# A transformer block on one core: first chunk's q and k stored straight into the attention layout, and the opening loads in the order of need

## Chip, core and metric

The kernel runs on one core of one Trainium2 chip. The metric is the device time of one execution, in microseconds (us). Besides it I quote the *span* of a profiled execution, which is some 2 us shorter, because the trace's times belong to it. The engines are named as the profile names them: PE (matrix), PEld (its weight load), DVE (vector), ACT (scalar), POOL (GpSimd), SP (SyncE, which here only issues DMAs), and the core's 16 DMA engines. The *granted clock* is the share of PE's full clock that the chip allowed it. Each timed execution is marked with a state, by its time and granted clock; those timed in rounds are all marked fast.

## The reference, cut to what matters

```python
def A(x, wqkv, wo):               # x is 2048 x 1024, 32 heads of 32
    q, k, v = split(x @ wqkv)     # wqkv is 1024 x 3072
    idx = pos[:, None] - 2 * arange(8)            # 8 keys, each 2 tokens further back
    attn = softmax(where(idx >= 0, q . k[idx] * scale, -1e9))
    return (attn . v[idx]) @ wo
def B(x, w_gate, w_up, w_down):   # 1024 -> 3584 -> 1024
    return ((x @ w_gate) * (x @ w_up)) @ w_down
h = x + A(layernorm(x), wqkv, wo)
return h + B(layernorm(h), w_gate, w_up, w_down)
```

All inputs and outputs are bfloat16.

## The kernel before

The tokens go through in four chunks of 512. For each chunk: layer norm, q/k/v projection on PE, attention on DVE, output projection ("wo"), second layer norm, gated feed-forward. PE should never stop. The attention and the later layer norms therefore run as *background generators*: after each group of matmuls (1.73 us) the program hands out credit, and background instructions are written into the program as long as the credit lasts. So the program order of DVE, ACT and SP work relative to PE's matmuls is fixed when the kernel is built.

```python
    def step(self, us):                                  # class Background
        self.now += us
        self.credit = min(self.credit + us * self.rate, 4.0)
        while self.credit > 0:
            item = next((i for i in self.items if i[0] <= self.now), None)
            ...
            got = next(item[1])                          # emit the generator's next piece
            if isinstance(got, tuple):
                item[0] = self.now + got[1]              # ("later", us)
            else:
                self.credit -= got
# ---- opening: what SP loads, in this order
    load_x0(0); load_x0(1)
    load_w(2)                 # weight block 0 in two halves
    load_x0(2)
    load_w(2)                 # weight block 1, ahead of the last x tile
    load_x0(3)
# ---- layer norm of a later chunk; the pool behind normalize() has 4 "ln" buffers
    def ln1(c):
        xts = load_x(c, "x", nc.gpsimd)
        yield "later", 8.0 if c < 3 else 5.0
        lnTs[c] = lnTp.tile([128, KO, TC], BF, tag="lnT", name=f"lnT1_{c}")
        def norm(t):
            ln = normalize(xts[t], mv4, rs4, t)          # DVE
            nc.sync.dma_start_transpose(lnTs[c][:, :, bass.ts(t, 128)], ln[:])
        for t in range(4):
            stats(xts[t], mv4, t)                        # DVE
            rstd_of(mv4, rs4, t, t + 1)                  # two steps on ACT
            ...
# ---- after each group of a projection: PSUM -> staging tile -> DRAM
    def evac_qkv(c, m, ps):                              # m: 0-7 q, 8-15 k, 16-23 v
        sg = t1k.tile([128, HB + TC], BF, tag="t1k", name=f"sg{c}_{m}")
        nc.scalar.copy(sg[:, HB:HB + TC], ps[:])
        hg = m % 8
        if m < 8:
            nc.sync.dma_start(qd[c][:, 4 * hg:4 * hg + 4, :, :].rearrange("c g d s -> (g d) c s"),
                              sg[:, HB:HB + TC].rearrange("p (c s) -> p c s", c=4))
            return
        nc.scalar.copy(sg[:, 0:HB], halo[:, m - 8, :])   # last 16 tokens of the chunk before
        if c + 1 < NCH:
            nc.scalar.copy(halo[:, m - 8, :], ps[:, TC - HB:TC])
        ...                                              # k and v likewise, to kd[c], vd[c]
# ---- and back, into the attention's layout (partition = sub-chunk x head)
    def load_qk(c):
        nc.gpsimd.dma_start(qD[:], qd[c].rearrange("c g d s -> (c g) d s"))
        nc.gpsimd.dma_start(kD[:], kd[c].rearrange("c g d s -> (c g) d s"))
    def attention(c):
        if c == 0:
            load_qk(0)
            load_v(0)
            yield "later", 7.0
        ...                                              # DVE: logits, softmax, weighted v
        nc.gpsimd.dma_start(od[c].rearrange("c g d s -> (c g) d s"), oD[:])
        ...                                              # od -> oT, the input of wo
# ---- program order
    qkv(0, range(1, 6))
    bg.add(ln1(3))
    start_attention(0)
    qkv(1, range(6))
    ...
    bg.finish(atts[0])
    bg.rate = 0.98
    nxt = wo_ln2(0)
```

PE's groups share 8 PSUM banks, and ACT frees a bank by copying it to `sg`. ACT also takes the layer norms' two inverse-square-root steps and the attention's exponential, in program order with those copies. And SP issues nearly everything: weights, stores, transposing DMAs.

## Time and profile before

| | before |
|---|---|
| time, median of 3 (lowest to highest) | 813.2 us (813.04 to 814.09) |
| profiled span, granted clock | 812.0 us, 0.995 |
| first projection at full width starts | 20.2 us |
| first attention product on DVE | 67.8 us |
| output projection of chunk 0 starts | 165.3 us |
| output projection of chunk 3 starts, after a wait of 4.9 us | 491.5 us |

The prediction shows the page and PE's waits. For what follows two more views are needed. First, SP's own row in the timeline: start, duration, queue, line, kind of DMA, target and source, count.

```profile
23.99 11.76 SPq L265 DMA_DIRECT2D qd<-sg  x8
...
54.43 6.66 SPq L209 DMA_TRANSPOSE lnT<-ln  x2
```

Eight stores took SP 11.76 us. A transposing DMA took SP 1.3 us at the least and 2.3 in the median; this pair, beside a load of the attention's inputs, took 6.66.

### The profile page before, as it was taken

The numbers are of one execution on the slowest core, as the hardware profiler recorded it, in microseconds if no ns is written. First come the engines' busy times: TensorE is split into PE (matmuls) and PEld (weight loads), VectorE is DVE, ScalarE is ACT, GpSimd is POOL, SyncE is SP. The second block draws the span as 40 slices with busy tenths as digits, with TensorE's granted clock in tenths as the row PEclk, the third lists the DMA queues.
The fourth block names the chain that finished last, engine by engine and source line by source line (L and its number), as shares of the span: only waits on it lengthen the run. The fifth ranks groups of instructions, "written<-read, shape, count | busy, mean of one in ns | idle before, by whom it ended". The sixth has DMA issues, their size and how long they took to land.

```text
span 812.0 us, 9901 instructions
## 1 busy us (share of the span) xinstructions
PE 795.3 (98%) x3700; PEld 410.6 (51%) x3769; DVE 551.8 (68%) x580; ACT 254.9 (31%) x562; POOL 171.8 (21%) x172
## 2 busy tenths in 40 slices
PE   7999999999999999999999997999999999999998
PEld 5444444444444444444444443466666666644445
DVE  4538999999899898999989945635646565311111
ACT  2554444314333310023333100245545555400000
POOL 3100000200001000002000001497878778100000
PEclk9999999999999999999999998999999999999999
DMA  9999564999855948848564596533323233465600
GB/s 310 317 254 235 123 192 105 260 281 253 289 161 189 316 117 277 281 132 288 182 199 145 136 312 141 129 99 84 103 54 104 55 102 90 152 219 182 187 27 27
DMA packets 194448, 144.32 MB, mean 178 GB/s; under 512 B 83424, under 2 KB 188000, under 8 KB 192352
## 3 DMA queue, kind: packets, MB, share of 16 engines
q1 hardware_dynamic: 189856, 118.51, 52.5%
q0 software_dynamic: 4544, 25.17, 8.9%
q8 instruction: 30, 0.49, 0.3%
q14 instruction: 18, 0.15, 0.1%
HBM read 114.29 MB, written 22.02 MB: 168 GB/s over the span
## 4 chain that ended last, share of the span: by engine, by line
PE 83%; issue 13%; DMA 3%; SPq 0%; POOL 0%; DVE 0%; ACT 0%; POOLq 0%
PE ps L343 19%; PE acc L524 18%; PE pg L343 7%; PE pu L343 7%; PE pz L575 6%; PE py L575 6%; PE px L575 6%; PE wo L466 5%; PE pv L575 3%; PE accl L514 3%; DMA od<-oD 1%; DMA x<-in_A_x_dram 1%; DMA oT<-od 1%; POOL oT L443 0%; SPq L226 0%
## 5 line engine op out<-in xcount | busy, mean ns | idle before, releaser
L343 PE MATMUL ps<-lnT,w_qkv 128*128 128x512 bf16 x721 | 158.4, 379 | 0.8
L343 PEld LDWEIGHTS <-w_qkv 128*128 128x128 bf16 x736 | 72.0, 98 | 86.6
L343 PE MATMUL pg<-lnT,w_wg 128*128 128x512 bf16 x439 | 105.0, 379 | 0.5
L343 PE MATMUL pu<-lnT,w_wu 128*128 128x512 bf16 x439 | 104.9, 379 | 0.4
L524 PE MATMUL acc<-w_wd,gs 128*128 128x512 bf16 x439 | 96.7, 379 | 0.5
L262 ACT CAST sg<-ps 128x512 bf16<-128x512 f32 x96 | 55.5, 586 | 65.3 <-PE ps L343 59.0
L506 DVE TENSOR_TENSOR h<-acc,h 128x512 bf16<-128x512 f32 x28 | 17.4, 682 | 81.8 <-PE acc L524 81.8
L428 DVE TENSOR_TENSOR pv<-vD,at 128x4096 bf16<-128x4096 bf16 x32 | 72.4, 2287 | 0.4
L388 DVE TENSOR_TENSOR prod<-qD,kD 128x4096 bf16<-128x4096 bf16 x32 | 72.3, 2285 | 0.0
L524 PEld LDWEIGHTS <-gs 128*128 128x128 bf16 x448 | 43.9, 98 | 52.8
L343 PEld LDWEIGHTS <-w_wg 128*128 128x128 bf16 x448 | 43.8, 98 | 52.9
L343 PEld LDWEIGHTS <-w_wu 128*128 128x128 bf16 x448 | 43.8, 98 | 52.9
L466 PE MATMUL wo<-w_wo,oT 128*128 128x512 bf16 x251 | 58.4, 392 | 5.1 <-DMA oT<-od 4.9
L491 ACT CAST gs<-pg 128x512 bf16<-128x512 f32 x56 | 32.8, 586 | 91.5 <-PE pg L343 88.1
L440 POOL DMA_DIRECT2D od<-oD x4 | 2.2, 544 | 251.0 <-DVE oD L438 153.5
L575 PE MATMUL px<-lnT,w_pair 128*128 128x512 bf16 x210 | 52.5, 380 | 0.9
L496 ACT CAST us<-pu 128x512 bf16<-128x512 f32 x56 | 32.8, 586 | 60.1 <-PE pu L343 54.4
L551 POOL TENSOR_TENSOR sw<-w_pair 128x512 fp32r<-128x512 bf16 x28 | 36.5, 1302 | 60.5 <-issue 32.2
L466 PEld LDWEIGHTS <-oT 128*128 128x128 bf16 x256 | 25.7, 101 | 37.4 <-DMA oT<-od 5.4
L178 ACT ACTIVATE rs<-mv,eps 128x1 f32<-128x1 f32 x32 | 9.4, 294 | 104.6 <-DVE mv L175 99.7
L553 POOL TENSOR_TENSOR sw<-w_pair 128x512 fp32r<-128x512 bf16 x28 | 36.9, 1318 | 0.0
L390 DVE TENSOR_TENSOR prod<-prod 128x4096 bf16<-128x4096 bf16 x16 | 36.6, 2289 | 0.3
(128 smaller groups left out, 1066.1 us busy)
## 6 DMA issues: line engine op xcount, KB each, us to landing
w_wd<-in_B_w_down_dram SPq DMA_DIRECT2D x32, 896.0 KB, 6.2
w_wg<-in_B_w_gate_dram SPq DMA_DIRECT2D x14, 1024.0 KB, 8.1
w_wu<-in_B_w_up_dram SPq DMA_DIRECT2D x14, 1024.0 KB, 6.0
w_wo<-in_A_wo_dram SPq DMA_DIRECT2D x8, 1024.0 KB, 6.9
w_pair<-in_B_w_gate_dram SPq DMA_DIRECT2D x14, 512.0 KB, 4.0
w_pair<-in_B_w_up_dram SPq DMA_DIRECT2D x14, 512.0 KB, 5.4
kd<-sg SPq DMA_DIRECT2D x32, 144.0 KB, 3.3
vd<-sg SPq DMA_DIRECT2D x32, 144.0 KB, 2.7
```

The costliest lines, as they stand in the source:

```text
L262: nc.scalar.copy(sg[:, HB:HB + TC], ps[:])
L343: nc.tensor.matmul(ps[:], lhsT=wt[:, ko, bass.ts(j, 128)], rhs=rhs[:, ko, :], start=(ko == 0), stop=(ko == KO - 1))
L388: nc.vector.tensor_tensor(prod[:, j], qD[:], kD[:, :, o:o + SUB], ALU.mult)
L390: nc.vector.tensor_tensor(prod[:, :, 0:16], prod[:, :, 0:16], prod[:, :, 16:32], ALU.add)
L428: nc.vector.tensor_tensor(pv[:, j], vD[:, :, o:o + SUB], at[:, w, None, :].to_broadcast((128, DH, SUB)), ALU.mult)
L466: nc.tensor.matmul(ps[:], lhsT=oTs[c][:, kk, t, :], rhs=wts["wo", c, hf][:, kk, :], start=(kk == 0), stop=(kk == KO - 1))
L491: nc.scalar.copy(gs[:], pg[:])
L496: nc.scalar.copy(us[:], pu[:])
L524: nc.tensor.matmul(acc[t][:], lhsT=hT[f][:, bass.ts(t, 128)], rhs=wts["wd", c, hf, b][:, j, :], start=(f == 0), stop=(f == NF - 1))
L551: nc.gpsimd.tensor_tensor(sw[:, 0], a21, a22, ALU.add)
L553: nc.gpsimd.tensor_tensor(sw[:, 2], a11, a21, ALU.subtract)
L575: nc.tensor.matmul(ps[:], lhsT=lhs[:, ko, :], rhs=rhs[:, ko, :], start=(fresh and ko == 0), stop=(ko == 3), skip_group_check=not fresh)
```

## The change

The intent has two parts. Chunk 0's q and k skip DRAM: each staged tile goes by four DMAs of four destination partitions each straight into `qD` or `kD`, half issued by SP and half by POOL, so that attention 0 can start sooner. And the opening's loads come in the order of need: the fourth x tile ahead of the second weight block, then weight blocks and x tiles alternating, all on SP. Along with it, layer norms and attention 0 move forward in program order, and the first transposed tile is split into two PSUM tiles.

```diff
+    qkv_in = {("q", 0): att.tile([128, DH, SUB], BF, tag="qD", name="qD0"),
+              ("k", 0): att.tile([128, DH, SUB + HB], BF, tag="kD", name="kD0")}
     def evac_qkv(c, m, ps):
...
+        if c == 0 and m < 16:
+            dst, o, n = (qkv_in["q", 0], HB, SUB) if m < 8 else (qkv_in["k", 0], 0, SUB + HB)
+            for cp in range(4):
+                (nc.sync if cp % 2 else nc.gpsimd).dma_start(
+                    dst[cp * 32 + 4 * hg:cp * 32 + 4 * hg + 4, :, :],
+                    sg[:, o + cp * SUB:o + cp * SUB + n])
+            return
... opening loads
     load_x0(0)
     load_x0(1)
-    load_w(2)
+    load_w0(0, 4)
     load_x0(2)
-    load_w(2)
+    load_w0(4, 4)
     load_x0(3)
... after the first projection
-    pump()
+    w1 = wpool.tile([128, KO, 512], BF, tag="w", name="w_qkv_1")
+    nc.gpsimd.tensor_copy(w1[:, 0, 0:1], x0[3][:, 0:1])
+    pump(2, w1)
+    xtiles[1] = load_x(1, "x", nc.sync)
+    pump(3)
+    xtiles[2] = load_x(2, "x", nc.sync)
+    pump(6)
... layer norm: no delay; chunk 3's transposes wait until chunk 0's projection is written
-        yield "later", 8.0 if c < 3 else 5.0
... program order
-    qkv(0, range(1, 6))
+    qkv(0, range(1, 4))
     bg.add(ln1(3))
     start_attention(0)
+    qkv(0, range(4, 6))
+    emitted.add("qkv0")
+    load_v(0)
     qkv(1, range(6))
     start_attention(1)
+    pump(pair_at)
```

More of the change, by code (lines that the diff above doesn't have):

```diff
@@ L154, with pump @@
     wts = {}
-    state = {"next": 0, "live": 0, "limit": pair_at}
-    def pump(eng=None):
+    state = {"next": 0, "live": 0, "limit": 1}
+    def pump(limit=None, wt=None):
+        state["limit"] = limit or state["limit"]
         while state["next"] < state["limit"] and state["live"] < 7:
             key, src, n = stream[state["next"]]
-            wt = wpool.tile([128, KO, 512], BF, tag="w", name="w_" + "_".join(map(str, key)))
-            (eng or nc.sync).dma_start(wt[:, 0:n, :], src)
+            if wt is None:
+                wt = wpool.tile([128, KO, 512], BF, tag="w", name="w_" + "_".join(map(str, key)))
+            nc.sync.dma_start(wt[:, 0:n, :], src)
             wts[key] = wt
+            wt = None
             state["next"] += 1
@@ L199, with transpose @@
     lnTs = {}
+    xtiles = {}
+    emitted = set()
     def ln1(c):
-        xts = load_x(c, "x", nc.gpsimd)
-        yield "later", 8.0 if c < 3 else 5.0
-        lnTs[c] = lnTp.tile([128, KO, TC], BF, tag="lnT", name=f"lnT1_{c}")
+        if c == 2:
+            xtiles[3] = load_x(3, "x", nc.gpsimd)
+        xts = xtiles[c]
         mv4, rs4 = ln_tiles(f"1_{c}")
+        lns = [None] * 4
+        def transpose(t):
+            if c not in lnTs:
+                lnTs[c] = lnTp.tile([128, KO, TC], BF, tag="lnT", name=f"lnT1_{c}")
+            nc.sync.dma_start_transpose(lnTs[c][:, :, bass.ts(t, 128)], lns[t][:])
         def norm(t):
-            ln = normalize(xts[t], mv4, rs4, t)
-            nc.sync.dma_start_transpose(lnTs[c][:, :, bass.ts(t, 128)], ln[:])
+            lns[t] = normalize(xts[t], mv4, rs4, t)
+            if c < 3:
+                transpose(t)
         for t in range(4):
@@ L219, in ln1, with load_w0 @@
         yield 0.55
-    def load_w(parts=1):
-        key, src, n = stream[state["next"]]
-        wt = wpool.tile([128, KO, 512], BF, tag="w", name="w_" + "_".join(map(str, key)))
-        for q in range(parts):
-            nc.sync.dma_start(wt[:, bass.ts(q, KO // parts), :], src[:, bass.ts(q, KO // parts), :])
-        wts[key] = wt
-        state["next"] += 1
-        state["live"] += 1
+        if c == 3:
+            while "qkv0" not in emitted:
+                yield "later", 1.0
+            for t in range(4):
+                transpose(t)
     x0 = [hp.tile([128, D], BF, tag="h", name=f"x0_{t}") for t in range(4)]
+    w0 = wpool.tile([128, KO, 512], BF, tag="w", name="w_qkv_0")
+    wts["qkv", 0] = w0
+    state["next"] += 1
+    state["live"] += 1
     def load_x0(t):
         nc.sync.dma_start(x0[t][:], x[bass.ds(t * 128, 128), :])
+    def load_w0(lo, n):
+        nc.sync.dma_start(w0[:, lo:lo + n, :], wqkv_v[:, lo:lo + n, 0:512])
     load_x0(0)
     load_x0(1)
-    load_w(2)
+    load_w0(0, 4)
     load_x0(2)
-    load_w(2)
+    load_w0(4, 4)
     load_x0(3)
@@ L263, in evac_qkv @@
         hg = m % 8
+        if m >= 8:
+            nc.scalar.copy(sg[:, 0:HB], halo[:, m - 8, :])
+            if c + 1 < NCH:
+                nc.scalar.copy(halo[:, m - 8, :], ps[:, TC - HB:TC])
+        if c == 0 and m < 16:
[5 more added lines that the diff above has]
+            return
         if m < 8:
@@ L267, in evac_qkv @@
             return
-        nc.scalar.copy(sg[:, 0:HB], halo[:, m - 8, :])
-        if c + 1 < NCH:
-            nc.scalar.copy(halo[:, m - 8, :], ps[:, TC - HB:TC])
         dst = (kd, vd)[m // 8 - 1][c]
@@ L298, in first_transpose @@
     def first_transpose(t):
-        pts[t] = psum.tile([128, KO, 128], BF, tag="mm", name=f"pt{t}")
-        for kk in range(KO):
-            nc.tensor.transpose(pts[t][:, kk, :], lns[t][:, bass.ts(kk, 128)], ident[:])
-        nc.scalar.copy(lnTs[0][:, 0:4, bass.ts(t, 128)], pts[t][:, 0:4, :])
+        for hf in range(2):
+            pt = psum.tile([128, KO // 2, 128], BF, tag="mm", name=f"pt{t}_{hf}")
+            for kk in range(KO // 2):
+                nc.tensor.transpose(pt[:, kk, :], lns[t][:, bass.ts(4 * hf + kk, 128)], ident[:])
+            pts[t, hf] = pt
+        nc.scalar.copy(lnTs[0][:, 0:4, bass.ts(t, 128)], pts[t, 0][:])
     def first_copy(t):
-        nc.vector.tensor_copy(lnTs[0][:, 4:8, bass.ts(t, 128)], pts[t][:, 4:8, :])
+        nc.vector.tensor_copy(lnTs[0][:, 4:8, bass.ts(t, 128)], pts[t, 1][:])
     def first_mm(t, kos):
@@ L331 @@
     first_mm(3, range(8))
-    order_after_x0 = const.tile([128, 1], BF)
-    nc.gpsimd.tensor_copy(order_after_x0[:], x0[3][:, 0:1])
-    pump()
+    w1 = wpool.tile([128, KO, 512], BF, tag="w", name="w_qkv_1")
[5 more added lines that the diff above has]
+    pump(6)
     bg.add(ln1(1))
@@ L356 @@
     oTs = {}
-    qkv_in = {}
     stored = set()
@@ L377, in attention @@
     def attention(c):
-        if c == 0:
-            load_qk(0)
-            load_v(0)
-            yield "later", 7.0
-        qD, kD, vD = qkv_in["q", c], qkv_in["k", c], qkv_in["v", c]
+        qD, kD = qkv_in["q", c], qkv_in["k", c]
         lg = att.tile([128, W, SUB], F32, tag="lg", name=f"lg{c}")
@@ L418, in attention @@
         prefetch_qk(c + 1)
+        while ("v", c) not in qkv_in:
+            yield "later", 1.0
+        vD = qkv_in["v", c]
         at = att.tile([128, W, SUB], BF, tag="at", name=f"at{c}")
```

## The prediction

> **What bounds the kernel now.** I read the page's busy shares first, then TensorE's (PE's) waits, then the chain that ended last around the longest of them, then the stretches by window, and last the timeline of the opening.
>
> The page, busy shares and slices:
> ```profile
> PE 795.3 (98%) x3700; PEld 410.6 (51%) x3769; DVE 551.8 (68%) x580; ACT 254.9 (31%) x562; POOL 171.8 (21%) x172
> ...
> PE   7999999999999999999999997999999999999998
> ...
> PEclk9999999999999999999999998999999999999999
> ```
> PE is the bound: 795.3 of 812.0 us. The two slices with a 7 (of 20.3 us each) are the opening and a place near 490 us; the second also has the only clock digit below 9. Removing every idle moment would give at most 16.7 us, 2.1%, plus what the slow clock costs. So "within 2%" is nearly settled at once; the question is how much of that the change gets.
>
> PE's waits, whole span:
> ```profile
> PE wo L466 <- DMA oT<-od: 4.9, 1, 4.9
> PE pt L301 <- DVE ln L183: 2.4, 3, 1.3
> PE ps L310 <- ACT lnT L302: 1.4, 4, 0.7
> ```
> One wait of 4.9 us, for the last chunk's attention output; the others, 3.8 us, lie in the first 20 us.
>
> The chain that ended last:
> ```profile
> 165.43 6.26 PE wo L466 x29
> 171.75 7.50 PE wo L466 x34
> ...
> 476.19 9.13 DMA od<-oD
> 485.90 5.53 DMA oT<-od
> 491.47 12.04 PE wo L466 x42
> 503.56 4.70 PE wo L466 x21
> ```
> VectorE (DVE) ends attention of chunk 3 at about 475; out to DRAM and back takes till 491.5, and PE stood from 486.6. Then the same 63 recorded matmuls that took 13.8 us at 165 take 16.7 us. Busy time by stretch says why:
> ```profile
> 477.00:486.60 9.60, 9.54 (x44) 4.15 (x43) 0.62 (x2) 0.00 (x0) 0.70 (x1) 1.00 1.01 369
> 486.60:491.50 4.90, 0.03 (x1) 0.03 (x2) 1.87 (x4) 0.00 (x0) 2.83 (x4) 0.88 1.09 334
> 491.50:508.00 16.50, 16.45 (x63) 6.96 (x65) 10.16 (x19) 1.49 (x6) 0.00 (x0) 0.83 0.46 88
> ```
> The third number from the end is the granted clock: 1.00, 0.88, 0.83. The wait costs 4.9 us and 2.8 us more of slow matmuls after it: **7.7 us**.
>
> Timeline of the opening:
> ```profile
> 12.94 0.69 DVE L287 BATCH_NORM_STATS2 st<-x 128x6 f32<-128x512 bf16 x1 [0.68 <-DMA x<-in_A_x_dram]
> ...
> 15.41 0.42 DVE L305 COPY lnT<-pt 128x512 bf16<-128x512 bf16 x1 [0.73 <-ACT lnT L302]
> ...
> 18.45 1.95 PE L310 MATMUL ps<-lnT,w_qkv 128*128 128x128 bf16 x32 [0.23 <-ACT lnT L302]
> ```
> The fourth x tile lands at 12.9 because a second weight block is ahead of it; DVE's half of each transposed tile's copy waits for ACT's half; the first projection ends at 20.4.
>
> **What the Trainium skill says.** "TensorE: Matmul & The Clock Gate", Part 1 (the HAM clock gate): idle for about a window of 3.4 us puts the array at half clock until it has been busy again. The trace agrees: after 4.9 us idle the clock is 0.83 for 16.5 us, while idles of up to 1.3 us in the opening leave it at 1.00. "DMA: Bandwidth & Descriptors", "Queues, rings and completion order": on each DMA engine descriptors are consumed in ring order. The trace agrees so far as the q stores of chunk 0, issued behind the weights at 24 us, took up to 3.6 us to issue and 10.3 us to land. Same page, "Why a DMA increments its semaphore by 16 and not by 1": the number of engines is the largest up to 16 that divides both sides' slowest dimension. The new stores write 4 partitions, so 4 engines each, on SyncE's (SP's) queue always the lowest ones. No store of the kernel before has such a shape; I take it as a risk.
>
> **The change part by part.**
>
> *Opening order.* Removed ahead of the fourth x tile: 1 MB of weights. At the 350 to 375 GB/s that the trace shows from 5 us on, x tiles 3 and 4 should land near 7.6 and 8.3 us (before: 9.25 and 12.9). Splitting the transposed tile in two PSUM tiles removes DVE's wait for ACT, 0.6 us in each of four rounds. Then PE's own work sets the rounds: 0.6 us of transposes plus 0.6 and 1.5 us of matmuls, 2.7 us, where before they took 4.3, 3.7 and 3.0. Following it through from the first normalization (5.6 us), second transposes at about 8.9, third at 11.6, fourth at 14.4, then 0.6 us of old matmuls and 1.95 us of new: the end is near 17.6 instead of 20.4. I take **2.6 us**. Block 1's weights now wait for the fourth x tile: issued about 8.6, 2 us latency, 2.9 us for 1 MB, so 13.5; needed at 17.6. Blocks 2 to 5 and the x tiles follow at 2.9 us each, ahead of need (6.9 us a block).
>
> *q and k past DRAM.* Removed: 16 stores to DRAM and two loads back (landing 6 to 11 us each). Added: 64 stores of 128 pieces of 256 or 288 bytes, half on SP, half on GpSimd (0.54 us of issue each there). Packets of that size took 18 to 19 ns each in this trace. PE waits for none of it directly. Before, attention 0 began at 67.8. Its place in the program moves from 65.4 to 44.7 us of the kernel's own background clock, 21 us earlier. Data allow less: SP's queue, busy without a gap from 24 to 65 us before, has 16 more issues (about 0.5 us each) and 8 transposing DMAs (1.3 to 4.4 us each) in the way. From 33 us, when the last weights have landed, 24 stores x 0.5 plus 8 x 1.8 is 26 us: about 59, landing 61. So attention starts near 61, some 7 us earlier, and DVE later makes up more: after 200 us it had 14 us of waits for ACT's evacuations, so it was held by program order, not by its own pace. In program order attention 3 ends at 437 instead of 472, before the chunk 2 output projection. Needed: at least 5 us earlier. So the 4.9 us wait goes, and its 2.8 us of slow clock: **7.7 us**.
>
> *Moved.* Layer norm of chunk 3 goes 19 us earlier in program order, and its four normalized tiles reuse buffers that the transposing DMAs of chunk 2 must first have read, on SP behind the stores. ACT takes its square-root steps between evacuations 16 to 18 of chunk 0. If they wait, evacuation stops, and with 8 PSUM banks PE stops eight groups later, at about 54 us. From the sums above, chunk 2's first two transposes land at about 50 and 53: just in time. If the four lowest DMA engines carry all SP stores (32 x 0.6 us of packets, plus 8 x 1.15 us of transposes and what remains of x), they land at 54 to 58, and PE loses 3 to 8 us. I charge **2.5 us** on average, and 0.5 us for a possible clock dip.
>
> Sum: 2.6 + 7.7 - 3.0 = 7.3 us; 813.2 - 7.3 = 806 us.
>
> **The rivals.**
> 1. *The new wait eats the gain.* As just told: the SP queue or its four engines hold chunk 1's or chunk 2's transposes, and PE waits at 52 to 60 us. For it: SP was already full there, and DVE waited 5.8 us for such transposes. Against: 2.2 MB of loads back no longer compete, and the longest transposes (3 to 6.7 us for two) fell beside those loads. At worst about 10 us: 813, and slower if the clock dips too.
> 2. *The chunk 0 output becomes late.* Attention 0 takes 84 us and its way through DRAM 13 us; PE wants it at 162.6, so it must start by about 65. Before, it had almost no slack (landed 165.2, used 165.3). With a start of 67 or later, PE waits some 2 us: 808 to 809.
> 3. *Only the opening counts*, because program order of the later work keeps attention 3 where it was: 810.5. Against: the order of the built program moves it 34 us.
> 4. *No new wait at all*: 813.2 - 10.3, about 803.
>
> **Range and chances.** Rival 4 and the sum give 803 to 806, rivals 2 and 3 808 to 811, rival 1 up to 813. I predict 806, with 802 to 812 for 8 in 10. Faster by 2% would need 797, more than all found: 0.02. Slower by 2% needs 829: 0.01.
>
> **What would show it.** Opening right: first full-width projection at about 17.6, no wait for the second weight block. Attention right: first product of q and k at 58 to 65 us, attention 3's store before 450, no wait for oT near 484, granted clock 1.00 in the chunk 3 output projection, which then takes 13.8 us. New wait right: PE idle between 52 and 60 us, with ACT waiting on layer-norm statistics or DVE on transposes. I would be wrong if attention started later than 66, if weight blocks 2 to 5 came late behind the stores (PE waiting at 24 to 46 us), or if the clock dipped elsewhere.

## More of the kernel before

Second, busy time by stretch: stretch, its length, busy time of PE, PEld, DVE, ACT and POOL with counts, then the granted clock, the DMA engines' share, and GB/s.

```profile
24.00:31.40 7.40, 7.40 (x35) 3.33 (x34) 0.00 (x0) 3.11 (x8) 0.00 (x0) 1.00 1.08 351
31.40:38.20 6.80, 6.75 (x33) 3.09 (x32) 5.80 (x12) 4.30 (x19) 2.17 (x4) 1.00 1.03 244
```

PE is busy throughout, at full clock, while the DMA engines move 351 and 244 GB/s.

## The result, and the profile after

The changed kernel takes **857.9 us** (median of 4, 857.35 to 858.41), against 813.64 us of the kernel before on the same chip (median of 4, 813.04 to 818.94). The ratio is 1.0529, with a 95% interval of 1.0484 to 1.0574: slower. Here and below a ratio is the mean time of one kernel's fast runs over that of the other's fast runs of the same rounds, so it isn't quite the ratio of the medians. The profiled span is 856.4 us at a granted clock of 0.974, so 44.4 us longer than before's 812.0.

The page of the changed kernel, busy shares and slices (21.4 us each):

```profile
PE 799.9 (93%) x3700; PEld 411.2 (48%) x3769; DVE 552.7 (65%) x580; ACT 253.2 (30%) x562; POOL 188.5 (22%) x194
...
PE   8645696899999999999999999999999999999998
...
PEclk9888798899999999999999999999999999999999
```

The loss sits in the first eight slices, up to 171 us. There PE has slices of 4, 5 and three times 6 tenths, where before all behind the first were nines, and six of the eight clock digits are 7 or 8. PE's two large waits, over the whole span (total, times, longest):

```profile
PE ps L376 <- ACT halo L286: 37.8, 5, 15.8
PE ps L376 <- DMA w_qkv<-in_A_wqkv_dram: 7.9, 2, 6.8
```

The first is a wait for a PSUM bank that ACT has not yet copied out; its last reader is the copy into `halo`. The second is a wait for weights. PE's timeline shows where they fall, the idle time before a row in brackets. First the opening:

```profile
17.46 13.98 PE L376 MATMUL ps<-lnT,w_qkv 128*128 128x512 bf16 x62
38.20 8.83 PE L376 MATMUL ps<-lnT,w_qkv 128*128 128x512 bf16 x32 [6.76 <-DMA w_qkv<-in_A_wqkv_dram]
```

The full-width projection starts at 17.46, but two blocks later PE stands 6.76 us for the fourth. Then the three long waits for ACT:

```profile
69.27 3.46 PE L376 MATMUL ps<-lnT,w_qkv 128*128 128x512 bf16 x8 [15.77 <-ACT halo L286]
...
93.19 3.45 PE L376 MATMUL ps<-lnT,w_qkv 128*128 128x512 bf16 x8 [10.50 <-ACT halo L286]
...
152.84 64.77 PE L376 MATMUL ps<-lnT,w_qkv 128*128 128x512 bf16 x282 [10.90 <-ACT halo L286]
```

Eight matmuls took 3.45 us after these waits where they take 1.73 at full clock. The clock records put the array at half clock from 34.9 to 41.8, 58.8 to 72.5, 86.1 to 96.4 and 144.2 to 157.8 us, around each of the four long waits.

Why ACT was late is read upstream. ACT's and DVE's rows at the end of the first wait:

```profile
67.91 0.29 ACT L181 ACTIVATE rs<-mv,eps 128x1 f32<-128x1 f32 x1 [37.26 <-DVE mv L178]
```

```profile
65.89 0.55 DVE L186 TENSOR_SCALAR ln<-x,mv,rs 128x1024 bf16<-128x1024 bf16 x1 [36.90 <-DMA lnT<-ln]
...
105.93 4.50 DVE L416 TENSOR_TENSOR prod<-qD,kD 128x4096 bf16<-128x4096 bf16 x2 [4.58 <-DMA vd<-sg]
```

ACT stood 37 us at a layer norm's inverse square root, waiting for DVE's statistics. DVE stood 37 us because the next normalized tile needs one of four buffers, and a transposing DMA (`lnT<-ln`) had not yet read it. The second DVE row is the first product of attention 0: at 105.9 instead of 67.8. And SP, which issues those transposes:

```profile
31.15 30.59 SPq L290 DMA_DIRECT2D qD<-sg  x12
61.84 1.37 SPq L217 DMA_TRANSPOSE lnT<-ln  x1
```

Twelve direct stores held SP for 30.59 us, 2.5 us each, where the eight stores to DRAM took 1.5 each, and the first transpose went out at 61.84 (before: 37.15). For most of that time the twelve did not move: the first packet of theirs (256 bytes, SP's queue) starts at 51.9 us. Ahead of them in the same queue stand the weights, whose last packet starts only at 57.6 us. The two stretches that were shown of before:

```profile
24.00:31.40 7.40, 7.35 (x34) 3.17 (x33) 4.01 (x10) 4.45 (x16) 2.37 (x5) 1.00 1.25 112
31.40:38.20 6.80, 0.04 (x2) 0.01 (x1) 0.00 (x0) 0.00 (x0) 3.25 (x6) 0.76 1.15 147
```

The DMA engines are as occupied as before, and move 112 and 147 GB/s in place of 351 and 244. The packet records say what sits there. Between 24 and 46 us the weights' packets of 1 KB took 118 ns (median), 49 between 17 and 24. Among them are 118 POOL packets of 4096 bytes at 488 ns, each collecting 16 of the stores' pieces of 256 bytes, and three times as many packets of 64 bytes. POOL's 4096-byte packets of x tiles take 175 ns.

The sum of the 44.4 us:

| stretch | before | after | difference |
|---|---|---|---|
| start to full-width projection | 20.23 | 17.46 | -2.77 |
| from there to chunk 0's output projection | 145.04 | 199.98 | +54.9 |
| from there to chunk 3's output projection | 326.2 | 321.2 | -5.0 |
| chunk 3's output projection to the next stage | 40.8 | 38.0 | -2.8 |
| the rest | 279.7 | 279.8 | +0.1 |

Of the 54.9 us, 46.3 are PE's waits (37.8 + 7.9, and 0.6 for a transpose), and 8.6 remain, which I put down to matmuls at half clock: PE worked through some 15 us of the four half-clock stretches, which makes 7.5. Before chunk 3's output projection PE no longer waits:

```profile
538.60 13.98 PE L497 MATMUL wo<-w_wo,oT 128*128 128x512 bf16 x63
```

### The profile page after: what moved, and what is told of

It is laid out like the page before. It is cut to its first block, busy times and chain, and to the rows that moved or that the text cites. A ratio compares the mean times of both kernels' runs of the same rounds, so it can differ in the third digit from the quotient of the medians.

```text
span 856.4 us, 9967 instructions
## 1 busy us (share of the span) xinstructions
PE 799.9 (93%) x3700; PEld 411.2 (48%) x3769; DVE 552.7 (65%) x580; ACT 253.2 (30%) x562; POOL 188.5 (22%) x194
## 4 chain that ended last, share of the span: by engine, by line
PE 72%; DVE 15%; SPq 6%; DMA 4%; issue 1%; ACT 1%; DVEq 0%; POOL 0%
PE acc L555 20%; PE pg L376 11%; PE pu L376 11%; PE pz L606 6%; PE py L606 6%; PE px L606 6%; PE wo L497 5%; DVE prod L416 4%; SPq L290 4%; PE pv L606 3%; PE accl L545 3%; DMA lnT<-ln 2%; DVE pv L459 2%; DVE prod L418 2%; DMA x<-in_A_x_dram 2%; SPq L163 2%
## 5 line engine op out<-in xcount | busy, mean ns | idle before, releaser
L376 PE MATMUL ps<-lnT,w_qkv 128*128 128x512 bf16 x721 | 167.0, 391 | 47.1 <-ACT halo L286 37.8
L497 PE MATMUL wo<-w_wo,oT 128*128 128x512 bf16 x251 | 55.6, 379 | 0.3
L582 POOL TENSOR_TENSOR sw<-w_pair 128x512 fp32r<-128x512 bf16 x28 | 36.7, 1310 | 75.7 <-DMA w_pair<-in_B_w_gate_dram 43.4
L186 DVE TENSOR_SCALAR ln<-x,mv,rs 128x1024 bf16<-128x1024 bf16 x16 | 8.8, 549 | 62.3 <-DMA lnT<-ln 59.2
```

The costliest lines, as they stand in the source:

```text
L376: nc.tensor.matmul(ps[:], lhsT=wt[:, ko, bass.ts(j, 128)], rhs=rhs[:, ko, :], start=(ko == 0), stop=(ko == KO - 1))
L497: nc.tensor.matmul(ps[:], lhsT=oTs[c][:, kk, t, :], rhs=wts["wo", c, hf][:, kk, :], start=(kk == 0), stop=(kk == KO - 1))
L582: nc.gpsimd.tensor_tensor(sw[:, 0], a21, a22, ALU.add)
```

## The experiments

My theory was a cascade, called N or T in the expectations: the narrow direct stores (four destination partitions, small pieces) hold up the weights and fill SP, SP's transposes come late, DVE waits for its four buffers, ACT waits for DVE, PE for ACT; and the late attention 0 then makes a further wait of the same kind. Rivals: G, the trouble is POOL's queue alone; Q, it is only the order on SP's queue; P, the trouble is the new places in program order (layer norms and attention earlier), whatever the stores; and, in the first batch, the new order of the opening loads. All kernels gave correct results.

| run | time (us) | span | PE's main waits (us) |
|---|---|---|---|
| changed kernel | 857.9 | 856.4 | ACT 37.8, weights 7.9 |
| a1_dram_again | 827.38 | 825.4 | ACT 13.0, transposes 4.1 |
| a2_all_sync | 869.58 | 867.7 | ACT 55.5 |
| a3_all_gpsimd | 904.03 | 902.2 | ACT 69.5, weights 20.1 |
| a4_opening_alone | 822.13 | 820.3 | attention output 8.1, transposes 3.6 |
| b1_one_partition | 871.03 | 869.2 | ACT 59.6 |
| f1_stores_last | 852.22 | 850.3 | ACT 32.7, weights 9.2 |
| d1_opening_keep_rest | 816.2 | 814.3 | attention output 8.4 |
| d2_rate | 807.93 | 805.8 | attention output 3.2 |
| p1_rate_alone | 809.04 | 814.7 | 8.4 behind late transposes, in this execution |
| g1_best | 809.82 | 808.9 | attention output 3.9 |
| h1_direct_alone | 841.45 | 839.6 | ACT 22.5, attention output 6.2 |
| q1_attention_later | 853.39 | 851.5 | ACT 24.7, weights 10.8, attention output 5.4 |

The kernel before ran beside each batch: 813.41 (7 runs), 814.14 (7), 813.97 (8) and 813.77 (1).

### a1_dram_again: the change without its direct stores

```diff
-        if c == 0 and m < 16:
-            ... four direct stores ...
-            return
...
     qkv(0, range(1, 4))
+    load_qk(0)
     bg.add(ln1(3))
```

> The changed kernel with q and k of chunk 0 sent through DRAM again; order of the program, opening and place of layer norm 3 as changed. Theory N (the narrow stores of 4 partitions are the cause: they fill 4 DMA engines and hold up weights and transposes): PE no longer waits for weight blocks 3 and 4 (7.9 us before), and of the 37.8 us of waits for evacuation under 8 us are left; 803 to 812 us. Rival P (the moved program order is the cause, layer norm 3 ahead of attention with its statistics between evacuations): the evacuation waits stay above 25 us and the time above 835 us.

Measured: 827.38 us (824.73 to 827.53), ratio 1.0162 [1.0145, 1.0179]. No wait for the fourth block. The direct stores thus cost 856.4 - 825.4 = 31 us of span. But this kernel is still 13.4 us above the kernel before, so the stores aren't all: opening order and program order lose as well. Its waits for ACT, 13.0 us, are of the same kind as the changed kernel's. The time lies between the two that were expected, so neither theory alone has all of it.

### a2_all_sync and a3_all_gpsimd: all direct stores on one queue

```diff
-                (nc.sync if cp % 2 else nc.gpsimd).dma_start(
+                nc.sync.dma_start(            # a2;  a3: nc.gpsimd.dma_start(
```

> All 64 direct stores on SyncE's queue. Theory N: no wait for weight blocks, because the stores stand behind them in the same ring; but the transposes stand behind twice as many stores (64 x 0.58 us of packets on 4 engines = 37 us), so the evacuation waits grow: 850 to 880 us. Rival G (GpSimd's software queue is slow, whatever the width): both waits shrink, under 830 us.

> All 64 direct stores on GpSimd's queue. Theory N: twice as many 4 KB packets of 0.5 us alternate with weight packets on the same 4 engines, so the wait for weight blocks 3 and 4 grows from 7.9 us to 15 to 25 us; the transposes share those engines, so evacuation waits stay above 10 us; 840 to 880 us. Rival Q (only SyncE's queue order matters, transposes behind stores): the evacuation waits vanish, under 822 us.

Measured: 869.58 and 904.03 us. With SP alone the weights are in time: no wait for them, their packets stay at 46 to 49 ns. But SP's stores hold the transposes up (first one at 50.5 us), and PE waits 55.5 us for ACT. From 38 to 50 us almost nothing but these stores moved: 2279 pieces of 256 bytes, 0.67 us a store, with the DMA engines busy to about 0.30, which fits four or five engines of 16. With POOL alone PE waits 20.1 us for weights and 69.5 for ACT, and the time is above the range that I expected. So Q falls, and so does G: without POOL it is worse than the mixed version. Each queue has its own way of losing: POOL's stores slow the weights, SP's stand before the transposes, and both delay attention 0.

### b1_one_partition: POOL's stores cut to one destination partition

```diff
+                for g in range(4):
+                    nc.gpsimd.dma_start(dst[p0 + g:p0 + g + 1, :, :], src[32 * g:32 * g + 32, :])
```

> As the changed kernel, but each GpSimd store writes one destination partition instead of four (four times as many stores, same bytes and pieces), so that its slowest dimension is 32 and it can run on 16 engines. Theory N (4 engines carry each narrow store and hold the weights' share on them): the small filler packets of 60 and 64 bytes vanish from the software queue, packets spread, and PE's wait of 7.9 us for weight blocks 3 and 4 falls under 2 us. Rival G (software-queue stores from SBUF hold up weights whatever their width): the wait stays at 6 us or more. The total is no test here, as 128 issues of about 0.7 us make attention late: 840 to 900 us.

Measured: 871.03 us. The packets of 64 bytes are gone, those of 4096 became packets of 512 at 28 ns, the weights' packets are back at 52 ns (both medians, 24 to 46 us), and PE waits for no later weight block:

```profile
24.00:31.40 7.40, 7.35 (x36) 3.33 (x35) 3.93 (x9) 4.45 (x16) 4.10 (x9) 1.00 1.12 294
```

That is 294 GB/s in place of 112. So the shape of POOL's stores, not the queue, made the weights late. One rival is left: b1 also slows POOL, which moved 0.26 MB between 24 and 46 us instead of 0.48. Against it, in the kernel before POOL moved 2.3 MB of wide loads there, and the weights' packets took 51 ns; a narrow store at that slower pace wasn't tried. The weights' lateness was also most of what held SP. With SP's own stores unchanged, b1 has:

```profile
25.69 14.82 SPq L293 DMA_DIRECT2D qD<-sg  x12
40.61 2.27 SPq L217 DMA_TRANSPOSE lnT<-ln  x1
```

The same twelve stores took 14.82 us instead of 30.59, and the first transpose went out 21 us earlier. It didn't save time: four times as many issues on POOL make q and k later still, attention 0 with them, and PE waits 59.6 us for ACT. PE's own wait for weights, 7.9 us, was the smaller part. What inside the DMA engines slows the weights is open: the records don't number the engine of a packet, and over half of the weights' packets were slow, not a quarter of them as the same four loaded engines out of 16 would suggest. I had argued the latter.

### f1_stores_last: SP's half of the stores behind the transposes of chunks 1 and 2

```diff
+                if cp % 2:
+                    deferred.append((to, src))        # issued by a generator behind ln1(1) to ln1(3)
+                else:
+                    nc.gpsimd.dma_start(to, src)
```

> As the changed kernel, but SyncE's half of the direct stores is issued after the transposes of chunks 1 and 2. Theory T (the 15.8 and 10.5 us that PE lost come from transposes queued behind narrow stores on SyncE): the evacuation waits before 100 us fall from 27 to under 6 us; the 7.9 us for weights stay, because GpSimd's half is as before; total 815 to 832 us. Rival P (the moved layer norm 3 is the cause): the second wait of about 10 us between 80 and 95 us, or one like it, stays.

Measured: 852.22 us, far above what was expected. The middle wait (10.5 us, ending at 93 in the changed kernel) is gone, although the layer norms kept their new places, which speaks against P for that wait. The first only fell from 15.8 to 10.65, because the transposes themselves now stand behind the weights while POOL's stores slow them:

```profile
30.64 38.51 SPq L217 DMA_TRANSPOSE lnT<-ln  x8
```

Eight transposes took SP 38.51 us with no store between them. And the third wait grew to 22.0 us.

### h1_direct_alone: the kernel before with the direct stores and nothing else

```diff
+        if c == 0 and m < 16:
+            ... the four direct stores of the change ...
+            return
...
-            load_qk(0)
```

> The kernel before with the direct stores alone: old opening, old places of the layer norms and of attention 0. Theory N (narrow stores on 4 engines are the main cost by themselves): the transposes of chunk 1 come late and PE waits for them or for evacuations by 10 to 35 us in all; 822 to 850 us. Rival P (they hurt only with weights behind the x tiles and layer norms early): 808 to 816 us.

Measured: 841.45 us, span 839.6, with waits for ACT of 22.5 us, the longest 16.4. So the stores alone, with every load, layer norm and attention in its old place, cost 27.6 us: P isn't needed for the bulk. PE waits for no later weight block here, so the weights' lateness isn't needed either. SP was held 30.80 us by its first 16 stores. I read this as back pressure from the DMA queue on its issuer; the profile shows the time on SP, not what it waits for. Their first packet moved at 25.6 us, so here, unlike in the changed kernel, they were for the most part slow while moving, beside POOL's stores and loads:

```profile
21.05 30.80 SPq L274 DMA_DIRECT2D qD<-sg  x16
72.46 3.57 PE L354 MATMUL ps<-lnT,w_qkv 128*128 128x512 bf16 x8 [16.40 <-ACT halo L270]
```

### a4_opening_alone and d1_opening_keep_rest: the opening alone

a4 has the change's opening with its early layer norms and its x tiles on SP. d1 has only the order of the first six loads and the split transposed tile:

```diff
-    load_w(2)
+    load_w0(0, 4)
     load_x0(2)
-    load_w(2)
+    load_w0(4, 4)
     load_x0(3)
...
+        for hf in range(2):
+            pt = psum.tile([128, KO // 2, 128], BF, tag="mm", name=f"pt{t}_{hf}")
```

> Only the opening of the change (order of loads, split transposed tile); q and k through DRAM, layer norm 3 and attention 0 at their old places. First projection ends at 17.5 instead of 20.4 us; the wait for chunk 3's attention output stays (5 to 8 us, as PE comes 2.9 us earlier) with its slow clock. Theory: 810 to 813 us. Rival (the reordered loads themselves delay weight blocks 2 to 5): PE waits at 24 to 46 us, above 815 us.

> The kernel before with the new order of the first six loads and the split transposed tile only; layer norms 1 to 3, their loads on GpSimd, and everything later as before. If the loss of the opening alone (822 us) came from the layer norms of chunks 1 and 2 moved forward, so that transposes met GpSimd's loads: first projection near 17.8 us, chunk 0 and chunk 3 output waits as before, 809 to 812 us. If it came from the order of the first loads: 818 us or more.

Measured: a4 822.13 us (820.76 to 822.6), ratio 1.0102 [1.0085, 1.0119]; d1 816.2 us (815.61 to 816.44), ratio 1.0018 [0.9987, 1.0049]. Both missed my expectation of a gain. The full-width projection did start earlier, by 2.4 us in a4 and 2.1 in d1. In d1 the gain is given back:

```profile
PE wo L467 <- DMA oT<-od: 8.4, 2, 5.0
```

The new one is 3.4 us before chunk 0's output projection, whose 63 matmuls then take 15.67 us; the 5.0 before chunk 3's are the old wait. DVE is not what is late: attention 0's output goes to DRAM at 150.9 instead of 152.3. But from there to PE's first use of it pass 15.9 us instead of 12.9, with the DMA engines at 375 GB/s between 155 and 160 us (292 before). In a4 attention 0 itself starts at 73.7, waiting for the load of k; before that, a transpose that ran beside POOL's load of q held SP, which stores k:

```profile
46.17 9.91 SPq L217 DMA_TRANSPOSE lnT<-ln  x1
```

One transpose took 9.91 us; those around it took 1.3.

### q1_attention_later: the change with attention 0 later in program order

```diff
-        bg.add(atts[c], bg.now + (5.0 if c == 0 else 0.0))
+        bg.add(atts[c], bg.now + (28.0 if c == 0 else 0.0))
```

> The changed kernel with one number changed: attention 0 stands 23 us of the background clock later in program order (start delay 28 instead of 5); stores, loads and opening stay. Question: is PE's third wait (10.9 us, ends at 152.8 in the changed kernel, for ACT's evacuation) caused by attention 0 starting at 105.9, far behind its place in the program, so that ACT meets its exponentials too early and stands there? Theory (cascade): with the later place ACT is no longer in front of PE: the two earlier waits (15.8 and 10.5, at 53 to 93) and the weights' 7.9 stay within 2 us, the third wait falls below 3 us; attention 0's own end, about 190 to 195, then makes the first output projection wait for its output, 2 to 10 us; the span falls by 3 to 14 us, to 842 to 853. Rival (the third wait comes from the narrow stores or from chunk 1's traffic directly, whatever the place of attention 0): the third wait stays within 2 us of 10.9, and the span within 2 us of 856.4, or grows by what attention 3 is now late at the last output projection (up to 8 us).

Measured: 853.39 us, span 851.5. The third wait, 10.90 us in the changed kernel, is gone; from the second wait PE runs through to chunk 0's output projection:

```profile
93.93 111.37 PE L376 MATMUL ps<-lnT,w_qkv 128*128 128x512 bf16 x494 [10.40 <-ACT halo L286]
205.14 13.98 PE L497 MATMUL wo<-w_wo,oT 128*128 128x512 bf16 x63
```

It arrives at 205.1 instead of 217.4, 12.3 us earlier: 10.9 of wait and some slow clock. The first product still came at 106.6, so attention was not faster; ACT merely no longer stood in front of PE. Of the 12.3 us, 7.4 are lost again: attention 3 is late once more, PE waits 5.4 us for its output, as in the kernel before, and the 63 matmuls behind it take 15.84 us instead of 13.98. So the third wait was indeed the late attention meeting its place in the program. In two points the expectation missed: the weights' wait rose to 10.8 us (expected within 2 of 7.9), and chunk 0's output made PE wait not at all (expected 2 to 10).

### d2_rate, p1_rate_alone and g1_best: the attention's pace instead

The 4.9 us before chunk 3's output projection, which the change was to remove, can also be removed by giving the background slightly more credit. p1 does only that, from 0.98 to 1.02; d2 is d1 with the same pace; g1 is d2 with chunk 3's layer norm one block earlier.

```diff
-    bg.rate = 0.98
+    bg.rate = 1.02        # p1, d2 and g1
```

> As the run before it in this list, and the pace at which attention is put between the matmuls from chunk 0's output projection on raised from 0.98 to 1.02: attention 3 ends at 447 instead of 472 in the kernel's own clock. Then the 4.9 us wait for chunk 3's attention output and the 2.8 us of slow clock after it vanish: 801 to 805 us. If VectorE cannot follow (it was 93% busy there), PE waits for it elsewhere: 808 us or more.

> The kernel before with one number changed: the pace of attention between the matmuls from chunk 0's output projection on, 0.98 to 1.02. If the 4.9 us wait for chunk 3's attention output and the slow clock after it cost 7.7 us, as predicted, this gives 805 to 807 us against 813.4, clock 1.00 in that projection. If the clock dip was no part of it: 808 to 809 us.

> As d2 (opening order, split tile, pace 1.02), and layer norm 3 one block of four groups earlier, so that VectorE is free when k of chunk 0 has come from DRAM. If the 3.2 us wait for chunk 0's attention output in d2 came from attention 0 starting behind layer norm 3, attention 0 starts about 3 us earlier (near 64.5 instead of 67.8 us), the wait goes: 801 to 804 us. If attention 0 is held by the load of k instead, no gain: 805 to 808 us.

Measured: d2 807.93 us (803.4 to 808.84), ratio 0.9904 [0.9855, 0.9953]; p1 809.04 (805.52 to 816.49), ratio 0.9917 [0.9862, 0.9971]; g1 809.82 (803.89 to 810.71, 6 runs), ratio 0.9925 [0.9887, 0.9963]. The three can't be told apart, and each median lies above the gain that was expected. In d2's profile the wait before chunk 3 is gone and 3.2 us before chunk 0 remain. In g1's, attention 0 begins at 69.1 (d2: 65.3) and that wait is 3.9 us, so the earlier layer norm 3 did not remove it.

p1's single executions spread over 11 us: 805.52, 805.87, 812.21 and 816.49. The profiled one is the slowest, and shows why. The chunk 3 wait is gone in it too, but a new one has come:

```profile
63.81 26.47 PE L343 MATMUL ps<-lnT,w_qkv 128*128 128x512 bf16 x113 [8.45 <-DMA kd<-sg]
```

SP's transposes ahead of it took 5.7 to 6.8 us each while the load of q took 19.2 us to land; DVE then waited 11.0 us for its buffers and ACT 11.7 us for DVE. That is the changed kernel's chain, in an execution whose opening is that of the kernel before. The kernel before has the chain too, and usually just enough slack in it. I have no trace of p1's fast executions, so the cause of the whole spread isn't shown.

## Why the prediction was wrong, by its own steps

*Opening order, 2.6 us: right.* 2.8 measured in the changed kernel, 2.4 in a4 and 2.1 in d1; no wait for the second weight block. But the prediction counted it as a gain of the end. d1 shows that it isn't one by itself: PE then waits for chunk 0's attention output (rival 2 of the prediction put it at some 2 us for an attention that starts at 67 or later; 3.4 and a slow clock measured with a start at 66.4, because the way through DRAM, taken as 13 us, took 15.9).

*The wait before chunk 3's output projection, 7.7 us: right.* 5.0 and 2.8 us went, the 63 matmuls took 13.98 us at full clock. (The 0.83 that the prediction reads over 16.5 us is a mean: the clock was half for 6.8 us, from 490.3.) The reason given, program order, also holds: q1 moves attention 0 back and the wait returns with 5.4 us, and two of p1's four executions, with the pace alone changed, are 8.1 and 8.4 us below the 813.97 of the kernel before beside them.

*"PE waits for none of it directly": wrong.* The direct stores were charged by count and issue time, "24 stores x 0.5 plus 8 x 1.8 is 26 us: about 59, landing 61". Twelve stores alone took SP 30.59 us; attention 0 started at 105.9. "Blocks 2 to 5 and the x tiles follow ..., ahead of need" was wrong too: the fourth block came 6.76 us late. (Both are among its own signs of being wrong.) The first error hangs on the second: the count begins "from 33 us, when the last weights have landed", and their last packet started at 57.6 us (36.1 in b1). The price of 18 ns a piece held on SP's queue (median 18 ns between 46 and 70 us); what was missing is what the stores do to other traffic. POOL's packets of 16 such pieces took 488 ns, 31 ns a piece, and while they were under way the weights' packets took 2.4 times as long. The page "DMA: Bandwidth & Descriptors" of the Trainium skill, section "Why a DMA increments its semaphore by 16 and not by 1", says how few engines such a store gets, four; POOL's packets agree, 8 of 4096 bytes and 24 of 64 bytes for one q store, which is two on each of four engines and two on each of twelve others. I quoted that section, and used it as a risk with a weight, not as the main number.

*The new wait, 3.0 us: this is the term of the sum that failed.* The mechanism was named in full, rival 1: SP late, transposes late, DVE's buffers, ACT's square roots, PE's banks. "At worst about 10 us" was the size. It measured 46.3 us of waits and 8.6 us that I put down to slow clock, 54.9. Three things were missing in it. The chain repeats: it stopped PE at 53, at 83 and, through the attention, at 142. Its delays come round again: the stores of a later group are written behind its evacuation, which waits for ACT. And the earlier places in program order, which I counted as a gain only, let ACT stand in front of PE for work whose data come late; q1 showed 12.3 us of that before chunk 0's output projection, 4.9 of them at the end.

In spans: the stores account for 31 of the 44.4 us (a1; 27.6 on the old kernel, h1), the opening with its early layer norms for 8.3 (a4), and the rest, 5.1, is the further move forward of chunk 3's layer norm and attention 0 (a1 against a4), which the attention's own gain at the end is already part of.

What stays open: what inside the DMA engines slows the weights beside POOL's stores, and why SP's stores were slow in h1 (1.9 us each), where the projection's weights were in time. No run on record has a direct store that spreads over all DMA engines on both queues, so whether the idea can be saved in another shape is not known. The best versions found keep the road through DRAM: p1, d2 and g1, some 1% faster than before.

## What to carry to other kernels

Removing a trip through DRAM is only worth it if what replaces it has no worse shape: here 16 wide stores and two loads, hidden behind matmuls, gave way to 64 narrow stores that were not hidden: one half slowed the weights, and the other stood in the queue that also issues the weights and the transposes. Before moving work forward in a program that is fixed at build time, ask which in-order engine will meet it before its data are there, and what that engine also does for the bottleneck. And a gain at the start of the critical engine lasts only as far as the next thing it waits for: pace that too, or it is handed back.

## What the Trainium skill lacked or had wrong

- "DMA: Bandwidth & Descriptors", section "Why a DMA increments its semaphore by 16 and not by 1": the number of engines fits (8 packets with data and 24 of 64 bytes for a q store of four partitions, as four engines and twelve would give). What is lacking is the price for others: the weights' packets went from 49 to 118 ns, the traffic from 351 to 112 GB/s, and cutting the same store to one partition brought them back to 52 ns and 294 GB/s.
- The same page, section "DMA Transpose (X-bar)", says nothing of a transpose's time beside other DMAs. Here one took SP 1.3 us at its fastest, 5.7 to 6.8 us beside a load of q (p1), and once 9.91 us (a4).
- "TensorE: Matmul & The Clock Gate", Part 1, has nothing wrong that these runs show: its idle window of about 3.4 us fits all 14 traces. Every idle of PE of 3.1 us or more brought half clock, those of 2.6 us or less did not, and each half-clock stretch before the program's end lasts a whole multiple of 3.41 us (6.83, 13.65, 10.24 and 13.65 in the changed kernel).
- No page that I read has the time that SP needs to issue a DMA behind a full queue: 0.5 us otherwise, here 2.5 us a store over 30 us behind late weights, and 1.2 us for the same stores in b1.
